# A written-out order of all engines replaced by another one (with its buffer, PSUM and engine tables) in a gated mix of two long convolutions

## The chip, the cores and the metric

The kernel runs on one core of one Trainium2 chip. A core has five engines that run at the same time, each through its own queue of instructions in a fixed order: TensorE (PE in the profile, its weight loads PEld) multiplies matrices into PSUM, VectorE (DVE) and ScalarE (ACT) work element by element on SBUF and PSUM, GpSimd (POOL) and SyncE (SP) here mostly issue DMAs. An instruction starts when it stands at the head of its engine's queue and the semaphores it waits for are set. The metric is the device time of one execution in microseconds (us), the median over several runs.

## What is computed

All arrays are bf16, the sequence has 2048 steps and there are 448 channels. The reference, cut to what matters:

```python
def _A_ref(u, A_re, A_im, B_re, B_im, C_re, C_im, log_dt, Dskip):
    dt = jnp.exp(log_dt)[:, None]
    logdA, dB = dt * (A_re + 1j * A_im), dt * (B_re + 1j * B_im)
    P = jnp.exp(logdA[:, :, None] * jnp.arange(L)[None, None, :])      # 448 x 256 modes x 2048
    K = jnp.einsum("dn,dnl,dn->dl", C_re + 1j * C_im, P, dB).real      # a filter of 2048 taps per channel
    return causal_convolution(u, K) + u * Dskip                        # by rfft, product, irfft of length 4096
def _B_ref(q, k, v, shift_k, ssm_k, ssm_D):
    kv = short_convolution_4_taps(k, shift_k) * v
    return q * (causal_convolution(kv, ssm_k) + kv * ssm_D)
x = A_u
g = sigmoid((x * gate_w).sum(-1, keepdims=True))
out = g * _A_ref(x, ...) + (1 - g) * _B_ref(x, k, v, ...)
```

## The kernel before, in words

**Tiling.** The 448 channels are four groups of 112. They lie on the partitions (32 per group) beside 32 residues of the sequence index, so that a sequence of 2048 is 32 x 64. The work on the filters goes through four channel quarters H = 0 to 3 of 28 columns x 4 groups (`NQG`, `NC`).

**Setup** builds constants with iotas on POOL and small DVE operations: tile `TP` serves as scratch, `G`, `s2_W` and `sa_R` (`s_W`, `sa_R` and `G` in the profile) are the transforms' matrices, `Wc` and `WcK` the masks. From dt, A, B and C it makes the modes' decay and phase (`hold`, q slots). Four of POOL's operations there fill 32x2048 elements each (method `turns`).

**The short convolution kv.** 448 matmuls in eight chunks of 56 multiply the transposed `k` (in tile `natu` and a slot) by a matrix `dg`, which is made on DVE in place in slot q1 from the `shift_k` load by two products (128x448 and 128x1344). Each chunk fills a PSUM room, and one DVE product `natv<-ps,natv` multiplies it by `v`. After the last chunk the four loads of `u` overwrite `natu`; the **gate** (112 matmuls `ps<-natu,q`, then tanh on ACT) reads `u`.

**A long convolution** of one quarter is a transform, a pointwise product and a transform back, all as matmuls: `spread` (`ps<-Wc,..`), `transform` (`ps<-q,s_W`), a swap of halves by eight SP DMAs (`q<-q`), two DVE products of 128x3584 (`q<-q,q`), `stage_a` (`ps<-sa_R,q`) and `stage_b` (`ps<-q,G`). After each PSUM room of results a copy (CAST or COPY `q<-ps`) brings it to a slot in bf16.

**A filter table T(H)** makes the filter K of one quarter: 16 exponentials on ACT (`q<-hold`), sines on ACT (`ET<-q`, with phases from DVE), a chain of DVE products and additions that builds the tables `TQ` and `TP` by doubling (`Part.tables`), with three accumulating POOL DMAs, then 448 small matmuls `ps<-TP,TQ` (`sums`), and a gather and spread on TensorE. Exponentials and sines use different function tables of ACT, and where the one follows the other the compiler puts an ACT_TABLE_LOAD between them.

**The plan** (`PLAN`) is T0 B0 B1 T1 B2 A0 T2 B3 A1 T3 A2, four mixes, A3 (A and B are the two convolutions of a quarter). T3 is made in two halves.

**What sets the order.** The Python code does not issue instructions: class `Order` records all 6479 calls in the order of the code, and `issue` (its line is L137, the one line that the trace has for all of them) then issues them as the string `ORDER` lists them (a number is a call, `a-b` a run of calls). Each engine's instructions are tied in that order, so no engine overtakes. Class `Places` hands out big buffers and PSUM rooms by two more strings: `SLOTS` gives for each request one of seven tiles q0 to q6 (128x3584 bf16), and `ROOMS` one of four PSUM tiles ps0 to ps3 (two banks each). A call that writes a slot or room waits until its earlier readers are done. Class `Sides` does the copies that DVE and ACT can both do: `SIDES` has one letter for each of 208 (V for DVE, S for ACT).

Calls by stage, for reading the diff: setup 0-226, kv 227-682 (its last product 682), loads of `u` 683-686, gate 687-804, T0 805-879, its sums 880-1327, gather and spread 1328-1448, B0 1449-1840, B1 1841-2237, T1 2238-2881 (sums 2313-2760), B2 2882-3278, A0 3279-3614, T2 3615-4259 (sums 3691-4138), B3 4260-4656, A1 4657-4992, T3 4993-5738, A2 5739-6074, mixes 6075-6078, A3 6079-6478.

Of the kernel before, what the change touches and what calls it, by code (L numbers as in the profile page):

```python
# [38 lines left out]
    "201031456232433120056615532041060303231061540604265013"  # L39
)  # L40
ROOMS = (
    "031230120122130132023010223312031201320001012121201100302332131110331210203301002313130323111031203103303210320132212000"
    "13111112310221033031032020012311212323010303033031323212102022201023121232131202010303130"
)
SIDES = (
    "SVSSSSSVSSSSSSSSSSSSSSSSSSSSSSSVSSSVSSVSSSSSSSSSSSSSSSSSSVVVVVSSSSSSSSSSSSSSSSSSSSSSSSSSSSSSSSSSSSSSSSSSSSSVVVVSSSSSSSSS"
    "SSSSSSSSSSSSSSSSSSSSSSVSSSSSSSSSSSSSSVSVVSVVSSSSSSVSSSSSSSSSSSVSSVVSSSSSSSSSVSVSVSSSVSSS"
)
ORDER = (
# [963 lines left out]
```

## Time and profile before

| what | value |
|---|---|
| median of 3 runs | 264.16 us (263.94 to 264.76) |
| profiled execution, first to last instruction | 257.9 us, so some 6.3 us of the measured time lie around it |
| DVE busy | 237.4 us in 378 instructions |
| TensorE busy | 208.9 us in 5631 matmuls |
| ACT busy | 199.5 us in 278 instructions |
| POOL busy | 30.5 us |
| DMA | 26.44 MB, mean 103 GB/s |
| first DVE operation, last DVE operation ends | 3.06 us, 247.6 us; what follows is the output's DMA |
| kv matmuls | 29.1 to 51.1 us |
| gate matmuls | 68.3 to 71.8 us |
| sums of T0, T1, T2 | 74.0 to 87.7, 121.5 to 132.5, 165.5 to 181.2 us |
| last matmul ends | 246.3 us |

All instructions have the line L137, so the profile is read by tiles: `q<-ps` is a copy out of PSUM, `TQ<-TQ,ET` a step of the filter's table chain, and so on. Buffer numbers are left out there (q stands for q0 to q6, ps for ps0 to ps3). Idle time of an engine stands with what ended it ("idle 11.67 <-PE ps": it waited for a matmul's room). Durations of DVE operations overlap by some hundredths of a microsecond, since the next one starts before the last one has written everything.

### The profile page before, as it was taken

How to read it: one execution, taken by the hardware profiler on the slowest of the kernel's cores; microseconds unless marked ns; L12 is line 12 of the kernel's file. 1: busy time of each engine (PE TensorE's matmuls, PEld its weight loads, DVE VectorE, ACT ScalarE, POOL GpSimd, SP SyncE). 2: the span in 40 equal slices, each digit the busy share in tenths (PEclk: the TensorE clock that was granted, in tenths of full speed). 3: DMA queues.
4: the chain of work that ended last, by engine and by line, in shares of the span. 5: the costliest groups of instructions: out<-in, count | busy, mean ns of one | idle time of the engine just before them, and what ended most of it. 6: DMA issues, size and time to landing. Idle time of an engine off the chain costs nothing.

```text
span 257.9 us, 12431 instructions
## 1 busy us (share of the span) xinstructions
PE 208.9 (81%) x5631; PEld 188.6 (73%) x5631; DVE 237.4 (92%) x378; ACT 199.5 (77%) x278; POOL 30.5 (12%) x81
## 2 busy tenths in 40 slices
PE   0634784988779999998889998989999998999820
PEld 0511484978669898997879887888899897998810
DVE  4999999999999999999999999988999999998830
ACT  2299993089979999999999999989999975653300
POOL 8970001200000002100000021000031120000000
PEclk9995596899979999999999999997999999999975
DMA  6999983499861347475043055600462375120088
GB/s 167 212 164 216 165 178 74 82 171 159 139 157 32 47 106 144 79 167 91 7 99 104 3 102 95 149 24 3 111 110 38 57 145 131 29 51 4 3 163 125
DMA packets 58917, 26.44 MB, mean 103 GB/s; under 512 B 49520, under 2 KB 57200, under 8 KB 58864
## 3 DMA queue, kind: packets, MB, share of 16 engines
q1 hardware_dynamic: 52192, 18.65, 39.5%
q0 software_dynamic: 2160, 5.51, 12.2%
q10 hardware_dynamic: 4512, 1.49, 3.0%
q8 instruction: 44, 0.72, 1.2%
q14 instruction: 9, 0.07, 0.1%
HBM read 8.17 MB, written 2.52 MB: 41 GB/s over the span
## 4 chain that ended last, share of the span: by engine, by line
DVE 61%; PE 17%; issue 6%; DMA 5%; ACT 5%; SPq 1%; POOL 1%; DVEq 0%; ACTq 0%; POOLq 0%
DVE TP L137 18%; PE ps L137 17%; DVE q L137 15%; DVE TQ L137 15%; DVE natv L137 5%; ACT q L137 3%; DMA TP<-TP 3%; DVE ET L137 3%; DVE G L137 2%; DVE RK L137 1%; SPq L137 1%; DMA q<-q 1%; ACT ET L137 1%; DMA sk<-in_B_ssm_k_dram 1%; DVE hold L137 1%
## 5 line engine op out<-in xcount | busy, mean ns | idle before, releaser
L137 ACT CAST q<-ps 128x1024 bf16<-128x1024 f32 (+4 forms) x151 | 126.6, 929 | 23.9 <-PE ps L137 23.1
L137 PEld LDWEIGHTS <-q 128*128 128x128 bf16 (+2 forms) x720 | 52.3, 147 | 13.5 <-DMA q<-in_A_A_re_dram 8.4
L137 DVE TENSOR_TENSOR TQ<-TQ,ET 128x896 bf16<-128x896 bf16 (+2 forms) x70 | 45.5, 687 | 0.1
L137 PEld LDWEIGHTS <-natu 128*32 128x32 bf16 (+1 forms) x560 | 30.6, 183 | 8.9 <-issue 7.2
L137 PE MATMUL ps<-TP,TQ 128*32 128x32 bf16 x1792 | 33.3, 240 | 4.1 <-DVE TQ L137 2.6
L137 PE MATMUL ps<-q,s_W 128*128 128x112 bf16 (+1 forms) x544 | 33.8, 214 | 3.5 <-ACT q L137 3.4
L137 PE MATMUL ps<-sa_R,q 128*128 128x128 bf16 x448 | 33.3, 229 | 2.4 <-DVE q L137 1.0
L137 PEld LDWEIGHTS <-TQ 128*32 128x32 bf16 x1792 | 30.1, 153 | 6.7 <-DVE TQ L137 3.1
L137 DVE TENSOR_TENSOR q<-q,q 128x3584 bf16<-128x3584 bf16 (+1 forms) x22 | 32.4, 1513 | 1.2 <-ACT q L137 1.2
L137 PEld LDWEIGHTS <-s_W 128*128 128x128 bf16 x544 | 28.2, 100 | 6.5 <-issue 4.5
L137 DVE TENSOR_TENSOR TP<-TP,ET 128x1792 bf16<-128x1792 bf16 (+3 forms) x25 | 31.4, 1275 | 0.1
L137 POOL DMA_DIRECT2D TP<-TP x15 | 13.1, 914 | 153.8 <-PE ps L137 89.6
L137 PEld LDWEIGHTS <-G 128*128 128x128 bf16 x1024 | 27.9, 96 | 4.3 <-issue 2.5
L137 PE MATMUL ps<-q,G 128*128 128x28 bf16 x1024 | 28.5, 175 | 1.4 <-ACT q L137 1.4
L137 ACT ACTIVATE q<-hold 128x224 bf16<-128x224 f32 x64 | 22.4, 414 | 5.0 <-DVE hold L137 5.0
L137 PE MATMUL ps<-q,natu 128*32 128x336 bf16 (+3 forms) x336 | 17.8, 334 | 5.7 <-DVE natv L137 4.2
L137 ACT ACTIVATE ET<-q 128x1344 bf16<-128x1344 int16 (+1 forms) x12 | 17.2, 1457 | 1.4 <-DVE q L137 1.3
L137 PE MATMUL ps<-q,q 128*32 128x336 bf16 (+3 forms) x112 | 17.8, 334 | 0.0
L137 PE MATMUL ps<-Wc,natu 128*64 128x128 bf16 x224 | 15.5, 285 | 0.6 <-DVE q L137 0.6
L137 ACT CAST RK<-ps 128x448 bf16<-128x448 f32 (+1 forms) x16 | 11.5, 742 | 5.4 <-PE ps L137 5.4
L137 DVE TENSOR_TENSOR TQ<-TQ 128x448 bf16<-128x448 bf16 (+2 forms) x35 | 15.3, 446 | 0.1
L137 DVE CAST q<-ps 128x1024 bf16<-128x1024 f32 (+3 forms) x13 | 12.6, 978 | 2.4 <-PE ps L137 1.4
(81 smaller groups left out, 276.6 us busy)
## 6 DMA issues: line engine op xcount, KB each, us to landing
q<-q SPq DMA_DIRECT2D x64, 112.0 KB, 3.1
TP<-TP POOLq DMA_DIRECT2D x9, 448.0 KB, 5.0
natv<-in_B_v_dram SPq DMA_DIRECT2D x4, 448.0 KB, 7.3
sk<-in_B_ssm_k_dram SPq DMA_DIRECT2D x16, 112.0 KB, 3.8
natu<-in_A_u_dram SPq DMA_DIRECT2D x4, 448.0 KB, 10.2
TP<-TP POOLq DMA_DIRECT2D x6, 224.0 KB, 3.8
out_dram<-natv SPq DMA_DIRECT2D x8, 112.0 KB, 4.6
out_dram<-natv ACTq DMA_DIRECT2D x8, 112.0 KB, 4.5
```

The lines of the kernel that those rows point to most:

```text
L137: ins = f(*args, **kw)
```

## The change

The calls are the same 6479, and so is all that they compute. The four strings are other ones: `SLOTS` and `ROOMS` place the buffers anew, `SIDES` has 22 letters V in place of 28, and `ORDER` issues the calls in another order on every engine. Some sums of a table (`1072-1135` before, `1072-1103` and `1104-1167` after, for instance) are cut at other places and stand among other groups of matmuls. The first lines are shown, and of `ORDER` those with the calls that the text speaks of:

```diff
@@ -36,71 +36,69 @@
 NSLOT = 7
 PLAN = (("T", 0), ("B", 0), ("B", 1), ("T", 1), ("B", 2), ("A", 0), ("T", 2), ("B", 3), ("A", 1), ("T", 3), ("A", 2), ("m", 0), ("m", 1), ("m", 2), ("m", 3), ("A", 3))
 SLOTS = (
-    "201031456232433120056615532041060303231061540604265013"
+    "011200652313211024454605234430165543031146525645042163"
 )
 ...
 SIDES = (
-    "SVSSSSSVSSSSSSSSSSSSSSSSSSSSSSSVSSSVSSVSSSSSSSSSSSSSSSSSSVVVVVSSSSSSSSSSSSSSSSSSSSSSSSSSSSSSSSSSSSSSSSSSSSSVVVVSSSSSSSSS"
-    "SSSSSSSSSSSSSSSSSSSSSSVSSSSSSSSSSSSSSVSVVSVVSSSSSSVSSSSSSSSSSSVSSVVSSSSSSSSSVSVSVSSSVSSS"
+    "SSSSSSSSSSSSSSSSSSSSSSSSSSSSVSSSSSSSSSSSSSSSSSSSSSSSSSSSSVVSVVSSSSSSSSSSSSSSSSSSSSSSSSSSSSSSSSSSSSSSSSSSSSVVVVSVSSSS"
+    "SSSSSSSSSSSSSSSSSSSSSSSSSSSVSVSSVSSSSSSSSSSVVVVVSSSSSSVSSSSSSSSSSSSSSSSSSSSSSSSSSSSSSSSSVVVS"
 )
 ...
 ORDER = (
-    "35 38 81 0 32-34 1 37 2 67-68 5 106 36 108 31 69 63 225 64 75 210 44 109 76 211 207 15 208 104 41 77 20 105 78 112 83 "
-    "107 74 6 71 202 70 66 212 72 209 73 221 214 50 82 30 65 111 219 110 79 17 140-155 215 84 216 116-117 203 222 91 204 "
 ...
-    "98-99 198 135 205 95-96 213 2257 206 125 200 101-102 136 826 47 92-93 126 838 128 97 138 218 114 341-396 843 835 139 "
 ...
-    "512-567 57 863 511 864 626-681 568 283 1466-1481 686 848 1449-1464 682 685 1483-1498 1465 684 850 1500-1507 1499 844 "
 ...
-    "1551 1535 868 2019-2026 1552 867 2246 1842 689-800 2027 1547 2018 1550 870 2239 1545 871 3615 872 879 1549 2259 877 "
-    "2037-2044 875 1621 2270 1136-1199 2269 2271 2260 2045 2264 1264-1327 2262 1845 2272 115 2263 2273 1640-1647 801 2265 "
-    "1008-1071 1648 2266 1880-1895 1897-1904 1896 880-943 1905 1649 1846-1861 802 1863-1878 2247 803 1072-1135 2243 2883 "
 ...
+    "2 15 71 1 19 67-69 75 77 116 70 104 72 109 207-208 105-106 108 111 209 112 225 76 33 214 63 28 212 60 210 107 110 "
 ...
+    "14 26 824 831-832 10 18 20 205 159 157 806 206 83 193-194 196 81-82 80 101-102 38 809 807 825-826 195 687 843 827 "
+    "198-199 89 130-135 137 136 98-99 74 833 45 139 123-124 120-122 125 39 95-96 200 2257 2238 50 129 812 46 839 814 127 "
+    "817 2240 128 819 828 197 834 92-93 138 73 47 49 846 126 808 848 835 847 850 94 849 852 840 103 841 512-567 48 97 "
 ...
+    "568 53 625 2253 55 54 398-510 341-396 855 52 682 201 57 2239 2244 2249 2258-2259 2243 41 511 227-283 683 685 "
 ...
+    "871 689-800 2037-2044 872 877 2241 1630 1648 867 2028-2035 801 2045 1844 864 869 1546 226 1631-1638 875 1613-1620 "
+    "1843 2036 802 876 1168-1231 1072-1103 1232-1295 2269-2270 2262 1639 944-1007 2271 2263-2266 2272-2273 2260 803 2251 "
+    "2267 1104-1167 1296-1327 3615 1329 3619-3620 1845 3626 880-943 1551 2274 1008-1071 3621 1552 3617 1880-1895 2261 "
 ...
```

What this does on the engines is shown at three places. In these lists q_77 to q_83 are the slots q0 to q6 and ps_84 to ps_87 the rooms ps0 to ps3; "x4" joins rows that read alike. The line is L135 after the change, as the strings are two lines shorter.

**DVE, the two products that make `dg`** (`q_78<-q_78,TP`, calls 74 and 73). Before they stand in the setup's first rows, among small constants:

```order
L137 TENSOR_SCALAR TP<-TP 128x32
L137 TENSOR_SCALAR TP<-TP 128x1
L137 TENSOR_SCALAR TP<-TP 128x64
L137 TENSOR_SCALAR TP<-TP 128x1
L137 TENSOR_TENSOR q_78<-q_78,TP 128x448
L137 TENSOR_SCALAR TP<-TP 128x1 x2
L137 TENSOR_SCALAR TP<-TP 128x4
L137 TENSOR_SCALAR TP<-TP 128x1
L137 TENSOR_TENSOR q_78<-q_78,TP 128x1344
L137 TENSOR_SCALAR minus<-TP 128x128
```

After, they stand behind the modes' products (`q_77<-TP`, `hold<-TP`) and among the products that make `G`:

```order
L135 TENSOR_TENSOR hold<-TP 128x8x2x28
L135 TENSOR_SCALAR G<-TQ,TP 128x64x32 x2
L135 TENSOR_TENSOR q_78<-q_78,TP 128x448
L135 TENSOR_SCALAR G<-TQ,TP 128x64x32
L135 TENSOR_TENSOR q_77<-TP 128x8x2x28
L135 TENSOR_SCALAR q_81<-hold 128x224
L135 TENSOR_SCALAR G<-TQ,TP 128x64x32 x3
L135 TENSOR_TENSOR hold<-TP 128x8x2x28
L135 TENSOR_TENSOR ET<-ET,q_83 128x3x448
L135 TENSOR_SCALAR G<-TQ,TP 128x64x32
L135 TENSOR_TENSOR q_78<-q_78,TP 128x1344
L135 TENSOR_TENSOR TQ<-hold,ET 128x896
```

So everything that DVE does in setup ahead of these rows now stands ahead of the matrix that the kv matmuls read.

**ACT, its first rows.** Before, the load of `shift_k` is ACT's first DMA, and two table loads stand ahead of the exponentials `q_81<-hold`:

```order
L137 DMA q_78<-in_B_shift_k_dram 128x1792
L137 DMA RK<-in_A_log_dt_dram 128x448
L137 ACT_TABLE_LOAD
L137 ACTIVATE TP<-TP 128x64
L137 ACT_TABLE_LOAD
L137 ACTIVATE TP<-RK 128x448
L137 ACTIVATE q_81<-hold 128x224 x2
L137 COPY RK<-ps_85 128x1792
L137 ACTIVATE q_81<-hold 128x224 x10
L137 ACTIVATE q_82<-q_82,quarter 128x4x224
L137 ACTIVATE q_83<-q_83,quarter 128x3x224
L137 ACT_TABLE_LOAD
```

After (from its sixth row on; two table loads stand ahead of these), there are table loads between the setup's sine for `sa_R` and the exponentials, and the load of `shift_k` has moved behind eight of ACT's operations on the exponentials and phases:

```order
L135 ACT_TABLE_LOAD
L135 ACTIVATE sa_R<-TP 128x256
L135 ACT_TABLE_LOAD
L135 ACTIVATE q_83<-hold 128x224 x4
L135 COPY RK<-ps_85 128x1792
L135 ACTIVATE q_83<-hold 128x224 x2
L135 ACTIVATE q_79<-q_79,quarter 128x3x224
L135 ACTIVATE q_83<-hold 128x224
L135 DMA q_78<-in_B_shift_k_dram 128x1792
L135 ACTIVATE q_83<-hold 128x224 x2
L135 ACTIVATE q_82<-q_82,quarter 128x4x224
L135 ACT_TABLE_LOAD
```

In all, ACT has 16 table loads after and 9 before. Ten of the 16 stand ahead of the first copy of B0's spreads; before, four of the nine do.

**ACT around T0's sums** (`RK<-ps` copies what they and no other matmuls leave, `gt` is the gate's tanh). Before, copies of B1's filter spreads (`q_78<-ps_84`, `q_78<-ps_85`) stand between the gate and the first copy of the sums:

```order
L137 ACT_TABLE_LOAD
L137 ACTIVATE q_82<-hold 128x224
L137 ACTIVATE gt<-ps_86 128x64
L137 ACTIVATE q_82<-hold 128x224
L137 ACTIVATE q_83<-hold 128x224
L137 COPY q_78<-ps_85 128x128x8
L137 ACTIVATE q_82<-hold 128x224
L137 ACTIVATE q_83<-hold 128x224
L137 ACTIVATE q_82<-hold 128x224
L137 COPY q_78<-ps_84 128x128x8
L137 ACTIVATE q_83<-hold 128x224 x2
L137 COPY RK<-ps_87 128x32x14
```

After, there are no copies of other matmuls between `gt` and the second copy of the sums, and those of B1's spreads come behind it:

```order
L135 ACT_TABLE_LOAD
L135 ACTIVATE ET<-q_83 128x3x448
L135 ACTIVATE ET<-q_77 128x3x448
L135 ACT_TABLE_LOAD
L135 ACTIVATE gt<-ps_86 128x64
L135 ACTIVATE q_82<-hold 128x224
L135 COPY RK<-ps_85 128x32x14
L135 ACTIVATE q_83<-hold 128x224 x6
L135 ACTIVATE ET<-ET 128x3x224
L135 ACTIVATE q_83<-hold 128x224 x3
L135 COPY RK<-ps_85 128x32x14
L135 COPY q_77<-ps_84 128x128x8
```

On TensorE the order has moved likewise: before, the sums of T0 stand in seven chunks of 64 with spreads, `transform` and `stage_a` groups between most of them; after, they stand in eight pieces of 64 or 32 with no other matmuls between.

More of the change, by code (lines that the diff above doesn't have):

```diff
@@ L38 @@
 SLOTS = (
-    "201031456232433120056615532041060303231061540604265013"
+    "011200652313211024454605234430165543031146525645042163"
 )
 ROOMS = (
-    "031230120122130132023010223312031201320001012121201100302332131110331210203301002313130323111031203103303210320132212000"
-    "13111112310221033031032020012311212323010303033031323212102022201023121232131202010303130"
+    "01231001012112100232101132130130121002331000202012103332132102313031210221220132300131001010302102012301102323203303"
+    "133000310220311032013302201202321002101113231232320031232013211122003013313201013310310202031"
 )
 SIDES = (
-    "SVSSSSSVSSSSSSSSSSSSSSSSSSSSSSSVSSSVSSVSSSSSSSSSSSSSSSSSSVVVVVSSSSSSSSSSSSSSSSSSSSSSSSSSSSSSSSSSSSSSSSSSSSSVVVVSSSSSSSSS"
-    "SSSSSSSSSSSSSSSSSSSSSSVSSSSSSSSSSSSSSVSVVSVVSSSSSSVSSSSSSSSSSSVSSVVSSSSSSSSSVSVSVSSSVSSS"
+    "SSSSSSSSSSSSSSSSSSSSSSSSSSSSVSSSSSSSSSSSSSSSSSSSSSSSSSSSSVVSVVSSSSSSSSSSSSSSSSSSSSSSSSSSSSSSSSSSSSSSSSSSSSVVVVSVSSSS"
+    "SSSSSSSSSSSSSSSSSSSSSSSSSSSVSVSSVSSSSSSSSSSVVVVVSSSSSSVSSSSSSSSSSSSSSSSSSSSSSSSSSSSSSSSSVVVS"
 )
 ORDER = (
[54 rows of a table removed]
[52 rows of a table added]
 )
```

91 rows, old and new, of the table ORDER are left out of this document.

## The prediction

> **What bounds the kernel now.** I read the page's head and chain first, then the busy time by stretches, then the waits, and last the timeline at the places that the change moves. From the page:
>
> ```profile
> span 257.9 us, 12431 instructions
> ...
> PE 208.9 (81%) x5631; PEld 188.6 (73%) x5631; DVE 237.4 (92%) x378; ACT 199.5 (77%) x278; POOL 30.5 (12%) x81
> ...
> DVE 61%; PE 17%; issue 6%; DMA 5%; ACT 5%; SPq 1%; POOL 1%; DVEq 0%; ACTq 0%; POOLq 0%
> ```
>
> DVE is busy for 92% of the span and is 61% of the chain that ended last. But the average hides that the limits differ by stage (columns: stretch, its length, then busy time of PE, weight loads, DVE, ACT and POOL):
>
> ```profile
> 40.00:60.00 20.00, 16.84 (x374) 15.51 (x375) 20.00 (x24) 8.24 (x13) 2.74 (x3) 0.83 0.77 120
> 80.00:200.00 120.00, 112.14 (x3125) 104.57 (x3122) 117.19 (x173) 116.41 (x164) 8.39 (x11) 0.99 0.40 81
> 100.00:180.00 80.00, 73.16 (x2124) 68.10 (x2122) 77.99 (x106) 77.57 (x106) 3.61 (x5) 0.98 0.39 82
> 200.00:246.00 46.00, 43.56 (x1349) 39.93 (x1348) 42.80 (x66) 26.48 (x35) 2.58 (x3) 1.00 0.29 61
> ```
>
> From 80 to 200 us DVE (117.2 of 120), ACT (116.4) and PE (112.1) are all close to full: ACT can make up at most 3.6 us there, and PE 6.8 between 100 and 180. From 40 to 60 and behind 200 ACT has room. Its largest idle time is one wait for kv:
>
> ```profile
> 52.48 3.99 ACT L137 CAST q<-ps 128x1024 bf16<-128x1024 f32 x4 [11.67 <-PE ps L137]
> ```
>
> So a delay of kv is one of the few things early on that ACT, and PE behind it, cannot hide: their work from there to 200 us is a row without gaps.
>
> **The change: kv starts later.** In the order before, `dg`'s two products are among DVE's first rows; in the new one the long one stands behind all products of the modes and seven of the eight `G` products. In the trace of before:
>
> ```profile
> 4.42 2.15 DVE L137 TENSOR_SCALAR TP<-TP 128x32 int32<-128x32 int32 x4
> 6.49 0.62 DVE L137 TENSOR_TENSOR q<-q,TP 128x448 bf16<-128x448 bf16 x1
> 7.02 1.56 DVE L137 TENSOR_SCALAR TP<-TP 128x1 int32<-128x1 f32 x3
> 7.54 1.55 DVE L137 TENSOR_TENSOR q<-q,TP 128x1344 bf16<-128x1344 bf16 x1
> 10.35 2.70 POOL L137 IOTA TP<- 32x2048 bf16 x3
> 10.50 1.87 DVE L137 TENSOR_SCALAR one<-TP 128x32 bf16<-128x32 int32 x1
> 15.56 2.90 ACT L137 ACTIVATE q<-hold 128x224 bf16<-128x224 f32 x10
> 31.59 2.08 DVE L137 TENSOR_SCALAR G<-TQ,TP 128x2048 bf16<-128x2048 bf16 x3
> 33.58 0.63 DVE L137 TENSOR_TENSOR TP<-TP,ET 128x896 bf16<-128x896 bf16 x1
> 34.11 0.86 DVE L137 TENSOR_TENSOR ET<-ET,q 128x1344 bf16<-128x1344 bf16 x1
> 37.32 0.63 DVE L137 TENSOR_TENSOR TP<-TP 128x896 bf16<-128x896 bf16 x1
> 40.89 1.09 DVE L137 TENSOR_TENSOR natv<-ps,natv 128x896 bf16<-128x896 f32 x1
> 42.89 0.63 DVE L137 TENSOR_TENSOR TQ<-hold,ET 128x896 bf16<-128x896 bf16 x1
> ...
> q<-in_B_shift_k_dram ACTq DMA_DIRECT2D x1, 448.0 KB, 5.4
> ```
>
> The seventh `G` product ends at 33.7 and the `ET` product, which is also ahead of `dg` now, at 35.0. Of what ran until then the 896 product (0.6) is not ahead; four small operations that ran later (0.2 to 0.3 each, together about 0.8) are. That is 35.2 us for the end of `dg`. The load of `shift_k`, now issued among ACT's first exponentials (they run until 18.5), lands 5.4 us later and is there by then. Unknown are POOL's big setup operations. While they run, small DVE operations last long: the one at 10.50 takes 1.87 us beside POOL's IOTA, and the groups at 4.42 and 7.02 show two more such stops. Before, the three cost DVE some 4.3 us together (2.15 + 1.56 + 1.87, less some 1.3 for seven or eight operations of 0.15 to 0.3); now the four POOL operations of about 1.9 us stand in one row at POOL's end, beside DVE's products of the modes. Bounds are no stop at all (4.3 us earlier) and all four in full (3.3 later). The operations are the same ones, so I take the cost near the old, 0.8 more for their standing in one row: kv starts at 36, where it started at 29.1.
>
> How long it then takes, by chunks of 56 matmuls (the last columns are the clock granted to PE, the DMA share and GB/s):
>
> ```profile
> 29.10:32.30 3.20, 3.18 (x60) 2.80 (x63) 3.20 (x8) 3.20 (x5) 0.00 (x0) 0.50 1.37 166
> 32.10:34.50 2.40, 2.40 (x71) 2.19 (x67) 2.40 (x5) 2.40 (x3) 0.00 (x0) 0.74 1.37 217
> 34.30:36.20 1.90, 1.90 (x75) 1.90 (x72) 1.90 (x4) 1.87 (x3) 0.00 (x0) 1.00 0.87 282
> ...
> 37.90:42.00 4.10, 0.00 (x0) 0.00 (x0) 4.07 (x6) 2.92 (x7) 1.01 (x1) 0.78 0.02 3
> 42.00:45.20 3.20, 3.17 (x60) 2.80 (x63) 3.20 (x3) 0.00 (x0) 0.00 (x0) 0.50 0.79 148
> 45.00:47.70 2.70, 2.70 (x71) 2.36 (x67) 2.70 (x5) 0.00 (x0) 0.87 (x1) 0.63 0.11 21
> 49.20:51.10 1.90, 1.90 (x72) 1.84 (x66) 1.90 (x3) 0.00 (x0) 0.86 (x1) 1.00 0.29 56
> ```
>
> Four chunks fill the rooms in 3.2 + 2.4 + 1.9 + 1.9 = 9.4 us (the first at a clock of 0.50, the fourth like the third). PE then waits 4.1 us for DVE's first `natv` product (40.89, ending 42.0) and starts again at 0.50. In the new order DVE has 17 products between `dg` and that one, table products but for one `G` (the first is the row at 42.89, the last but one that at 37.32, and each takes 0.38 to 1.10). That is 11.6 us of durations, or 10.6 from start to start as neighbours overlap by some 0.06: the first `natv` product ends at 47.7, and PE, done with four chunks at 45.4, waits 2.3. With the slow clock again after that wait, the other four take 3.2 + 2.7 + 1.9 + 1.9 = 9.7 and kv ends at 57.4 (51.1 before): 6.3 us late.
>
> The Trainium skill ("TensorE: Matmul & The Clock Gate", Part 1) says that the clock falls back to half only after an idle window of about 3.4 us. The 4.1 us wait agrees; a 2.3 us wait would keep the clock by it, and kv would end 2.1 us earlier than I say, for 267.4 in place of 269.5 at the end. No run so far shows a wait of that length.
>
> What follows kv:
>
> ```profile
> 51.12 10.31 SPq L137 DMA_DIRECT2D natu<-in_A_u_dram  x4
> 68.27 3.56 PE L137 MATMUL ps<-natu,q 128*32 128x64 bf16 x112 [0.26 <-ACT q L137]
> 73.98 2.19 PE L137 MATMUL ps<-TP,TQ 128*32 128x32 bf16 x128 [1.65 <-DVE TQ L137]
> ```
>
> The loads of `u` go into the tile that kv reads, so they move by 6.3, and so does the gate, 68.3 to 74.6. PE idled 1.65 us before T0's sums for DVE's table; that gap takes up some, so PE's work is **4.7 us** late from there. With the bounds (kv start 4.3 + 0.8 earlier to 2.5 later, clock 2.1) it is between 0 and 7. DVE itself is hardly late: its operations until the end of T0 are the same apart from waits for kv's last two chunks (1 to 4 us).
>
> **T0's sums in one row.** 448 matmuls with none between give ACT nothing to copy for 448 x 2.19 / 128 = 7.7 us (by the row at 73.98), and B1's spreads come after. ACT has exponentials of T1 and T2 for some of it. The cost is between 0 and 3 us, and I take **1.0**, since most of it is work that ACT must do at some time.
>
> **Copies and table loads.** From the groups, with shapes kept apart, and the timeline of ACT at the gate:
>
> ```profile
> L137 DVE CAST q<-ps 128x1024 bf16<-128x1024 f32 x6 | 7.3, 1222 | 2.1 <-PE ps L137 1.1 <-ACT ET L137 1.0
> ...
> L137 ACT CAST q<-ps 128x1024 bf16<-128x1024 f32 x64 | 64.0, 1044 | 16.6 <-PE ps L137 16.2 <-DVE TP L137 0.3
> ...
> L137 ACT ACT_TABLE_LOAD x9 | 11.5, 1283 | 3.3 <-PEq L997 1.7 <-DVE q L137 1.4
> ```
> ```profile
> 79.02 0.60 ACT L137 CAST q<-ps 128x512 bf16<-128x512 f32 x1
> 79.63 1.28 ACT L137 ACT_TABLE_LOAD   x1
> 80.93 0.39 ACT L137 ACTIVATE q<-hold 128x224 bf16<-128x224 f32 x1
> 81.22 0.20 ACT L137 ACTIVATE gt<-ps 128x64 f32<-128x64 f32 x1
> ```
>
> DVE gives up three copies of 1024 (3 x 1.22), two smaller ones (some 0.65 each, by ACT's 0.60 for 512) and a tiny one (0.2), and makes one phase copy 0.1 longer: 5.1 us, or 4.7 as its operations overlap. ACT gains 4.4 us for the same copies. Its table loads go from 9 to 16, 7 x 1.28 = 9.0 us, but ten of the 16 stand ahead of B0's first copy (four before), where ACT had 11.67 us of idle time: six cost nothing, and one, 1.3 us, falls into the full stretch. If kv came early, that cover would be gone and they would cost up to 7.7. So ACT has 4.4 + 1.3 = 5.7 more there, and 3.6 of idle time against it: **2.1**.
>
> **The rest of the order.** B2's transforms and products come later, T1's and T2's sums stand among other matmuls, slots and rooms are other ones. All of that leaves each engine's amount of work as it is and can only change who waits for whom. The nearest row is what PE waits for ACT in all:
>
> ```profile
> PE ps L137 <- ACT q L137: 5.5, 18, 0.8
> ```
>
> I take nothing, with 5.5 us either way as the bounds.
>
> **What can be made up.** PE has 6.8 us idle between 100 and 180. It can use them only where DVE and ACT are ahead of it; ACT is not, so I take a third, **-2.5** (between 0 and -6.8). DVE's own 4.7 us less I count at nothing: DVE then waits for PE and ACT, which are late next.
>
> Sum: 4.7 + 1.0 + 2.1 - 2.5 = 5.3. The profiled execution of before has 257.9 us and some 6.3 around it, which is the median of 264.16; so 263.2 of span and **269.5 us**. Behind the last matmul stands the output's DMA, whose issues are not moved.
>
> **Rivals.**
>
> *DVE alone decides.* It is the chain's 61%, and it has 4.7 us less. If kv's lag is swallowed (POOL's stops vanish, the clock stays, so that the gate ends before DVE's table does), DVE's time counts: 264.2 - 4.7 + 1 to 3 for the waits at kv's end = 260.5 to 262.5. It decides if PE's lag at T0's sums is below about 1.7 us, which the gap of 1.65 can hide. Against it stands the row of windows: ACT is as full as DVE, and it gets the work that DVE loses.
>
> *They cancel.* Lag and lighter DVE give the same time within 0.8 us: 263.4 to 265.
>
> *ACT becomes the bound.* The lag of 4.7, T0's sums at their upper bound of 3, and 5.7 of added work with nothing made up: 13.4, at the most 277.6; I take 273 to 278. It decides if ACT stays over 97% busy until 200 us and waits elsewhere no longer. Against it: behind 200 ACT has 19.5 us idle.
>
> *A table load costs more than its own time.* It would, if ACT had to run empty around it. The rows at the gate show 0.01 us ahead of the load and 0.02 behind, and the overlap of 0.1 us that neighbours have (80.93 + 0.39 against 81.22) is lost: 7 x 0.1 = 0.7 us, a time inside the forecast's range. The Trainium skill ("ScalarE: Activation LUTs", What ACT_TABLE_LOAD costs) gives 1283 ns, as here, and about 1380 ns of drain besides. By that rule the seven would cost 9.7 us more than I say, at the worst 279; the rows at the gate show no gap of that size.
>
> **How the numbers follow.** Differences under 0.3% (0.8 us) could not be told from no change. The forecast (265 to 273) gets 0.56, DVE alone 0.20, cancelling 0.06, ACT as the bound 0.16, the dearer load 0.02. Faster is 0.20, same 0.06, slower 0.74. The range that leaves out no more than 2 in 10 reaches from 261 into ACT's case, 276; the forecast's own is 265 to 273.
>
> **What would show it.** In the profile after: first kv matmul near 36, a wait on `natv` of 2 to 3 us in mid-kv, kv's end near 57, gate near 75, T0's sums behind it in one stretch of 8 to 9 us (7.7 and some waiting); 16 table loads on ACT; DVE busy near 232 with more idle time "<-ACT q" and "<-PE ps"; the span near 263. I am wrong if kv starts before 32, if the gate comes before DVE's last `TQ`, or if PE is fuller than before between 100 and 180.

## The result, and the profile after

| kernel | median of its runs | against the kernel before on the same chip |
|---|---|---|
| after the change | 272.75 us (272.25 to 273.86) | 1.037 (1.031 to 1.043) |
| after the change, on another chip | 272.83 us | 1.033 (1.026 to 1.040) |
| before, run again as the kernel under test | 262.79 us | 1.001 (0.997 to 1.005) |

The change makes the kernel slower by 3.3 to 3.7%, some 9 us. The kernel before has medians of 261.8 to 264.1 us on these chips. Some executions take over 1% longer than the others of their kernel; the medians here leave them out, and the traces of the first cut and of the relief in the tail are of such executions. In each execution of which a span is known, the time is the span and some 1.8 us (272.25 for a span of 270.5 after, 262.56 for 260.7 before). So the execution profiled for the prediction, with its span of 257.9, was a quick one of about 259.7 us, and the "6.3 us around it" of the two texts above are not there. Below, the profile of before taken again (span 260.7) is compared with that of after; the shown one would make the difference 3 us larger than it is.

The page after:

```profile
span 270.5 us, 12420 instructions
...
PE 208.2 (77%) x5631; PEld 188.2 (70%) x5631; DVE 237.8 (88%) x372; ACT 214.6 (79%) x291; POOL 31.1 (11%) x81
...
PE 39%; ACT 16%; DVE 15%; SPq 10%; DMA 8%; issue 7%; POOL 0%; ACTq 0%; DVEq 0%; POOLq 0%
...
L135 ACT ACT_TABLE_LOAD x16 | 20.5, 1283 | 1.5 <-PEq L995 1.2
L135 DVE TENSOR_SCALAR q<-hold 128x224 int32<-128x224 f32 x40 | 16.3, 455 | 1.0 <-PE ps L135 1.0
```

and of before, taken again:

```profile
PE 208.5 (80%) x5631; PEld 188.0 (72%) x5631; DVE 237.7 (91%) x378; ACT 199.7 (77%) x278; POOL 30.6 (12%) x81
...
L137 DVE TENSOR_SCALAR q<-hold 128x224 int32<-128x224 f32 x40 | 10.1, 299 | 0.2
```

DVE has lost six copies and is as busy as before (237.8 against 237.7): its 40 phase operations `q<-hold` alone have grown from 10.1 to 16.3 us. DVE's share of the chain has fallen to 15% (48% in before again), PE leads it, and no engine is full. So the time has gone into waiting and into operations that stand still. The next table counts it on DVE, from its rows: when each filter table's last DVE operation ends, and how long DVE idled since the mark ahead of it (us; T3b is the second half of T3).

| DVE's mark | before again: end, idle | after: end, idle | lag |
|---|---|---|---|
| end of T0's table | 73.9, 3.7 | 78.2, 3.8 | 4.3 |
| end of T1's table | 124.2, 3.3 | 129.2, 7.0 | 5.0 |
| end of T2's table | 168.6, 0.2 | 177.4, 1.8 | 8.8 |
| end of T3b's table | 220.9, 2.9 | 229.2, 1.6 | 8.3 |
| last DVE operation | 250.5, 2.7 | 261.4, 9.4 | 10.9 |

Three stretches make the lag: 4.3 us up to the end of T0's table, 4.5 between there and T2's, 2.6 behind T3b, with 0.5 gained between T2 and T3b. A mark also moves when other operations are put ahead of it: between T1's and T2's the lag grows by 3.8 us, the idle time by 1.6.

PE's amount of work is a second measure (columns as in the prediction's windows). Before again and after:

```profile
0.00:80.00 80.00, 52.02 (x1159) 43.15 (x1160) 76.11 (x139) 56.77 (x81) 19.54 (x67) 0.87 0.89 152
0.00:200.00 200.00, 162.15 (x4243) 145.46 (x4245) 190.57 (x305) 170.78 (x241) 27.98 (x78) 0.94 0.60 109
```
```profile
0.00:80.00 80.00, 42.91 (x828) 35.45 (x832) 75.22 (x128) 60.22 (x85) 20.22 (x67) 0.97 0.78 139
0.00:200.00 200.00, 152.86 (x4033) 137.40 (x4034) 186.59 (x290) 174.05 (x239) 27.34 (x76) 0.97 0.56 107
```

By 80 us PE has done 9.1 us less than before, by 200 us 9.3 less. On PE the whole difference is there ahead of T0's sums, and from then on it neither grows nor shrinks much.

**The start.** POOL's four big operations now stand in a row, and DVE's small ones stand still beside them. POOL and then DVE after:

```profile
9.09 1.82 POOL L135 MEMSET TP<- 32x2048 bf16 x1
10.97 1.99 POOL L135 IOTA TP<- 32x2048 bf16 x1
13.00 1.83 POOL L135 MEMSET TP<- 32x2048 bf16 x1
14.89 2.70 POOL L135 IOTA TP<- 32x2048 bf16 x2
```
```profile
8.52 6.45 DVE L135 TENSOR_SCALAR q<-hold 128x224 int32<-128x224 f32 x6
14.89 2.00 DVE L135 TENSOR_SCALAR TP<-TP 128x4 f32<-128x4 int32 x1
15.02 2.71 DVE L135 TENSOR_SCALAR q<-hold 128x224 int32<-128x224 f32 x2
17.65 0.60 DVE L135 TENSOR_TENSOR hold<-ps,TP 128x448 f32<-128x448 bf16 x1
...
30.74 0.61 DVE L135 TENSOR_TENSOR q<-q,TP 128x448 bf16<-128x448 bf16 x1
...
37.58 1.55 DVE L135 TENSOR_TENSOR q<-q,TP 128x1344 bf16<-128x1344 bf16 x1
```

Nine operations, by the before row worth 0.15 to 0.3 us each, take DVE from 8.5 to 17.7. ACT waits for `hold` until 18.29, where its exponentials started at 13.45 before. Before again, ACT from there to its first sine into `s_W`:

```profile
13.45 0.67 ACT L137 ACTIVATE q<-hold 128x224 bf16<-128x224 f32 x2 [5.13 <-DVE hold L137]
...
20.15 1.28 ACT L137 ACT_TABLE_LOAD   x1
21.45 1.32 ACT L137 ACTIVATE ET<-q 128x1344 bf16<-128x1344 int16 x1
...
28.03 1.04 ACT L137 ACTIVATE s_W<-ps 128x1024 bf16<-128x1024 int16 x1
```

and after:

```profile
18.29 1.23 ACT L135 ACTIVATE q<-hold 128x224 bf16<-128x224 f32 x4 [7.42 <-DVE hold L135]
...
24.15 1.28 ACT L135 ACT_TABLE_LOAD   x1
...
32.03 1.28 ACT L135 ACT_TABLE_LOAD   x1
33.32 0.67 ACT L135 ACTIVATE q<-hold 128x224 bf16<-128x224 f32 x2
...
37.88 1.28 ACT L135 ACT_TABLE_LOAD   x1
39.17 1.02 ACT L135 ACTIVATE s_W<-ps 128x1024 bf16<-128x1024 int16 x1
```

That sine empties the PSUM room into which kv's first chunk goes. PE's first kv matmul, before again and after:

```profile
29.12 0.60 PE L137 MATMUL ps<-q,natu 128*32 128x448 bf16 x3 [1.49 <-ACT s_W L137]
```
```profile
40.24 0.60 PE L135 MATMUL ps<-q,natu 128*32 128x448 bf16 x3 [7.17 <-DMA natv<-in_B_v_dram]
```

It starts 0.05 us after the sine's end in both (28.03 + 1.04, 39.17 + 1.02). The row after names a DMA, a load of `v`, which landed at 40.23 and which these matmuls don't read. The transposed `k`, which they do read, was late as well: its transfer stood in SP's queue until 30.21 (17.11 before), as the slot q2 that it fills was T0's until ACT had read the phases. The trace doesn't have its landing; the second and third experiment tell it from the sine. kv thus starts 11.1 us later, where 6.9 were predicted.

**kv itself** went faster than predicted. First chunk, fourth, the wait and the second half, after (columns as in the prediction's windows):

```profile
40.20:43.20 3.00, 2.96 (x57) 2.54 (x60) 2.97 (x8) 3.00 (x3) 0.00 (x0) 1.00 1.38 159
...
47.20:48.80 1.60, 1.50 (x55) 1.37 (x48) 1.50 (x4) 1.60 (x6) 0.00 (x0) 1.00 0.04 10
48.80:50.60 1.80, 0.00 (x0) 0.00 (x0) 1.80 (x4) 1.80 (x5) 0.00 (x0) 1.00 0.00 0
50.60:52.20 1.60, 1.52 (x49) 1.52 (x52) 1.60 (x3) 1.57 (x3) 0.00 (x0) 1.00 0.00 0
...
55.60:57.30 1.70, 1.70 (x68) 1.70 (x60) 1.70 (x4) 0.00 (x0) 1.01 (x1) 1.00 0.03 10
```
```profile
50.68 0.43 PE L135 MATMUL ps<-q,natu 128*32 128x448 bf16 x3 [1.98 <-DVE natv L135]
```

The four first chunks take 8.5 us, the wait 2.0, the four last 6.8: no slow clock behind the wait. kv ends at 57.5, 7.1 later than before again (50.4) and where the prediction had it, but by luck, as errors of opposite sign met. The clock in the first of these rows needs care: it reads 1.00, but 57 matmuls in 3.0 us are as slow as before's 60 in 3.2 at 0.50.

**From kv to T1.** `natu<-in_A_u` follows kv and takes longer to land (median 11.3 us, 9.7 in before again), so that the gate, at 77.5 (74.6 predicted), is 9.2 us late where kv's end is 7.1 late. T0's sums run from 83.5 to 93.6. ACT waits for the gate, and its sines for T1, queued behind, are late for DVE:

```profile
77.50 3.56 PE L135 MATMUL ps<-natu,q 128*32 128x64 bf16 x112 [5.33 <-DMA natu<-in_A_u_dram]
```
```profile
81.11 0.21 ACT L135 COPY gx<-ps 128x64 f32<-128x64 f32 x1 [6.16 <-PE ps L135]
...
84.33 1.28 ACT L135 ACT_TABLE_LOAD   x1
85.62 2.55 ACT L135 ACTIVATE ET<-q 128x1344 bf16<-128x1344 int16 x2
```
```profile
86.98 0.86 DVE L135 TENSOR_TENSOR ET<-ET,q 128x1344 bf16<-128x1344 bf16 x1 [4.51 <-ACT ET L135]
```

### The profile page after: what moved, and what is told of

The parts are those of the page before. It is cut to its first block, busy times and chain, and to the rows that moved or that the text cites. A ratio compares the mean times of both kernels' runs of the same rounds, so it can differ in the third digit from the quotient of the medians.

```text
span 270.5 us, 12420 instructions
## 1 busy us (share of the span) xinstructions
PE 208.2 (77%) x5631; PEld 188.2 (70%) x5631; DVE 237.8 (88%) x372; ACT 214.6 (79%) x291; POOL 31.1 (11%) x81
## 4 chain that ended last, share of the span: by engine, by line
PE 39%; ACT 16%; DVE 15%; SPq 10%; DMA 8%; issue 7%; POOL 0%; ACTq 0%; DVEq 0%; POOLq 0%
PE ps L135 39%; ACT q L135 11%; SPq L135 10%; DVE q L135 6%; DMA natu<-in_A_u_dram 5%; DVE TQ L135 3%; DVE TP L135 3%; ACT ET L135 2%; ACT L135 1%; DMA q<-q 1%; DMA sk<-in_B_ssm_k_dram 1%; DVE RK L135 1%; DMA xfd<-q 1%; DVE natv L135 1%; ACT TQ L135 1%
## 5 line engine op out<-in xcount | busy, mean ns | idle before, releaser
L135 ACT CAST q<-ps 128x1024 bf16<-128x1024 f32 (+4 forms) x156 | 130.3, 927 | 19.1 <-PE ps L135 17.8
L135 PEld LDWEIGHTS <-q 128*128 128x128 bf16 (+2 forms) x720 | 51.7, 148 | 16.9 <-DMA q<-in_A_A_im_dram 6.7
L135 DVE TENSOR_TENSOR TQ<-TQ,ET 128x896 bf16<-128x896 bf16 (+2 forms) x70 | 45.3, 684 | 0.3
L135 PE MATMUL ps<-TP,TQ 128*32 128x32 bf16 x1792 | 34.1, 241 | 4.7 <-issue 3.3
L135 PEld LDWEIGHTS <-natu 128*32 128x32 bf16 (+1 forms) x560 | 29.0, 180 | 11.6 <-issue 10.1
L135 DVE TENSOR_TENSOR q<-q,q 128x3584 bf16<-128x3584 bf16 (+1 forms) x22 | 32.4, 1511 | 5.3 <-DMA q<-q 4.0
L135 PEld LDWEIGHTS <-TQ 128*32 128x32 bf16 x1792 | 30.7, 154 | 7.2 <-issue 5.0
L135 PE MATMUL ps<-q,s_W 128*128 128x112 bf16 (+1 forms) x544 | 32.2, 210 | 4.3 <-ACT q L135 4.1
L135 PE MATMUL ps<-sa_R,q 128*128 128x128 bf16 x448 | 33.2, 232 | 2.1 <-DVE q L135 1.6
L135 PEld LDWEIGHTS <-s_W 128*128 128x128 bf16 x544 | 27.1, 98 | 6.9 <-issue 5.1
L135 DVE TENSOR_TENSOR TP<-TP,ET 128x1792 bf16<-128x1792 bf16 (+3 forms) x25 | 31.5, 1271 | 0.1
L135 PEld LDWEIGHTS <-G 128*128 128x128 bf16 x1024 | 28.1, 96 | 4.2 <-issue 1.5
L135 PE MATMUL ps<-q,G 128*128 128x28 bf16 x1024 | 28.9, 174 | 1.2 <-ACT q L135 1.1
L135 POOL DMA_DIRECT2D TP<-TP x15 | 13.0, 868 | 146.0 <-PE ps L135 71.9
L135 ACT ACTIVATE q<-hold 128x224 bf16<-128x224 f32 x64 | 21.9, 406 | 7.5 <-DVE hold L135 7.4
L135 PE MATMUL ps<-q,natu 128*32 128x336 bf16 (+3 forms) x336 | 15.3, 301 | 9.1 <-DMA natv<-in_B_v_dram 7.2
L135 PE MATMUL ps<-TP 128*128 128x512 bf16 x16 | 7.7, 611 | 12.9 <-POOL TP L135 4.5
L135 ACT ACTIVATE ET<-q 128x1344 bf16<-128x1344 int16 (+1 forms) x12 | 17.4, 1458 | 0.1
L135 DVE TENSOR_SCALAR q<-hold 128x224 int32<-128x224 f32 x40 | 16.3, 455 | 1.0 <-PE ps L135 1.0
L135 PE MATMUL ps<-Wc,natu 128*64 128x128 bf16 x224 | 16.3, 287 | 0.1
L135 DVE TENSOR_TENSOR TQ<-TQ 128x448 bf16<-128x448 bf16 (+2 forms) x35 | 15.2, 444 | 0.2
## 6 DMA issues: line engine op xcount, KB each, us to landing
natu<-in_A_u_dram SPq DMA_DIRECT2D x4, 448.0 KB, 11.3
```

The lines of the kernel that those rows point to most:

```text
L135: ins = f(*args, **kw)
```

## The experiments

The theory at the outset was the prediction's: a late kv, by POOL's row on DVE and by what stands ahead of `dg`, sets the time, and what comes behind T0's sums is neutral. Its rivals were that the order behind T0 costs as much, that the table loads do, or that the measured execution of before was an odd one. In the diffs below only the numbers that move are shown; all else in the strings is as it was.

**POOL's big operations apart again, as before** (81, 83, 82 and 80 are the four).

```diff
 ORDER = (
-    "2 15 71 1 19"
+    "81 2 15 71 1 19"
...
-    "107 110 223-224 221"
+    "107 110 223 83 224 221"
...
-    "815 811 9 160-175"
+    "815 811 9 82 160-175"
...
-    "84 86 85 3 8 62"
+    "84 86 85 3 80 8 62"
...
-    "806 206 83 193-194 196 81-82 80 101-102"
+    "806 206 193-194 196 101-102"
```

> The new order with one thing undone: POOL's four big setup operations (32x2048) stand again early and apart in POOL's queue, as before, and not in one row at its end. In the profile of the new order DVE's small operations on the phases stand still beside them from 8.5 to 17.7 us, and the exponentials on ACT start at 18.3 (13.45 before). Theory 'a late start' (POOL's row holds the exponentials, these hold the last transpose of k and dg, so kv, the gate and T0's sums are late, and the lag stays to the end): exponentials near 13.5, kv's first matmul near 36, 268 to 269.5 us (3 to 4.5 less than the new order's 272.75). Rival 'the later order' (the lag of the start is made up, and what costs is how the stages from T1 on are interleaved): kv is earlier, the time 271.5 to 273.

Measured 269.5 us (268.1 to 271.2), 1.030 (1.025 to 1.035). DVE's phase operations are back at their old time and T0's table ends at 76.3 in place of 78.2:

```profile
L135 DVE TENSOR_SCALAR q<-hold 128x224 int32<-128x224 f32 x40 | 9.3, 280 | 2.5 <-PE ps L135 1.4 <-ACT ET L135 1.1
```

The exponentials start at 16.49 and kv at 38.45, both 1.8 earlier; 13.5 and 36 were expected. So POOL's row holds 1.8 of the exponentials' 4.8 us, and the other 3.0 stay. Others of DVE's operations now stand still, as they did before the change, so that its busy time falls by 2.9 us in all (237.8 to 234.9). Some 1 to 2 us of that reach the end (1.037 and 1.033 against 1.030, with intervals that overlap, so that this is likely and not certain).

**`k`'s transpose and `dg` early.** The transpose gets slot q4 in place of q2, T1's first phases change to q2 and move behind T0's, and `dg`'s products (74, 73) stand ahead of 843, a copy for T0's table.

```diff
 SLOTS = (
-    "011200652313211024454605234430165543031146525645042163"
+    "011400652313211024452605234430165543031146525645042163"
...
 ORDER = (
-    "837 2256 822 2254 830"
+    "837 822 830"
...
-    "21 2255 176"
+    "21 176"
...
-    "195 687 843 827"
+    "195 687 74 73 843 827"
...
-    "98-99 74 833"
+    "98-99 833"
...
-    "95-96 200 2257 2238"
+    "95-96 200 2256 2254-2255 2257 2238"
...
-    "92-93 138 73 47"
+    "92-93 138 47"
```

> The new order with kv's inputs undone: the last transpose of k gets slot q4 and T1's first phases get q2 (their first three DVE operations move behind T0's), so the transpose no longer waits for T0's sine on ACT; and dg's two products stand ahead of T0's table products. POOL's row stays. 'A late start': kv's first matmul moves from 40.2 to 33 to 36, its end from 57.5 to 51 to 54, the gate by 4 to 6; DVE's table for T0 still ends near 78, so T0's sums start 3 to 4 earlier: 268.5 to 270.5 us. 'The later order': 271.5 to 273.

Measured 273.76 us, 1.046 (1.042 to 1.049). kv was to start at 33 to 36 and started later instead, so the run says nothing on an early kv, but it shows what kv waits for:

```profile
29.65 2.10 DVE L135 TENSOR_TENSOR q<-q,TP 128x448 bf16<-128x448 bf16 x2 [3.27 <-DMA q<-in_B_shift_k_dram]
```
```profile
43.57 0.60 PE L135 MATMUL ps<-q,natu 128*32 128x448 bf16 x3 [13.23 <-ACT s_W L135]
```

`dg` was there at 31.8 and the transpose issued at 16.4, and kv still waited until 43.6, for ACT's sine into `s_W`, which the 3.3 us that DVE stood for `shift_k` had put off. So neither `dg` nor `k` was what kv waited for last.

**Both edits together.**

> Both of these together. 'A late start': kv starts near 30 to 32, T0's sums near 75 to 77, and the time falls to 264.5 to 267 us. 'The later order': 270 to 272, little less than with one of them.

Measured 270.88 us, 1.038 (1.031 to 1.044). kv starts at 39.94, right behind the sine into `s_W` (38.86 and 1.02 long), with `dg` done 11.8 us before:

```profile
39.94 0.62 PE L135 MATMUL ps<-q,natu 128*32 128x448 bf16 x3 [9.16 <-ACT s_W L135]
```

As kv moved by only 0.3 us, this run tells nothing between the two theories. In all fourteen profiles, those of the runs below included, the first kv matmul starts 0.05 to 0.06 us behind the end of that sine.

**The start as before, cut at four places.** The first 1171, 1786, 3095 or 5445 calls of the new order are put in the order, the slots, the rooms and the sides that they have in the kernel before; the rest stays as after. Each begins so, and goes over to the new strings at its place:

```diff
 ORDER = (
-    "2 15 71 1 19 67-69 75 77 116 70 104 72 109 207-208 105-106 108 111 209 112 225 76 33 214 63 28 212 60 210 107 110 "
+    "35 38 81 0 32-34 1 37 2 67-68 5 106 36 108 31 69 63 225 64 75 210 44 109 76 211 207 15 208 104 41 77 20 105 78 112 83 "
...
```

> The first 1171 calls that the new order issues (setup, kv, gate, T0's table and the first spreads of B0 and B1) stand in the order, slots, rooms and engines that they had before the change; all behind them stands in the new order. 'A late start': 263 to 266.5 us, close to the kernel before. 'The later order': at or above 269, since T0's sums in one row, B1's late spreads and everything from T1 on are still the new order's.

> The first 1786 calls of the new order (setup through T0's sums, B1's filter spreads and the begin of T1's table) stand as before the change, what is behind them in the new order. With the first 1171 calls as before, the ratio was 1.019. Theory 'contiguous sums' (T0's sums in one row and B1's spreads behind them hold ACT and DVE up): 1.005 to 1.010. Rival 'T1 and later': 1.015 to 1.022, no gain against the earlier cut.

> The first 3095 calls as before (through T1's sums and the begin of B2), the rest in the new order. 'T1 and later', if it is the stretch of T1 where B2's transforms wait behind T1's sums: 1.000 to 1.007. If the cost is the last stretch (DVE's waits for A2's swaps and for A3's copies, 3.5 + 2.5 + 1.2 us idle in the new order): 1.010 or more.

> The first 5445 calls as before (through most of T3), only the tail in the new order. If the waits of the tail are its own: 1.008 to 1.015. If they only pass on a lag from earlier: 0.997 to 1.004.

| as before up to | median, us | ratio to before | T1's, T2's, T3b's table ends, last DVE operation |
|---|---|---|---|
| 1171 calls, ahead of T0's sums | 266.58 | 1.019 (1.013 to 1.025) | 124.7, 174.8, 226.5, 259.1 |
| 1786, through T0's sums | 266.32 | 1.013 (1.008 to 1.018) | 122.3, 171.4, 224.8, 257.6 |
| 3095, through T1's sums | 268.64 | 1.021 (1.018 to 1.025) | 124.8, 173.9, 226.9, 259.0 |
| 5445, through the sums of T3's first half | 266.35 | 1.012 (1.009 to 1.016) | 124.3, 168.7, 226.7, 255.4 |

Putting the start back takes 1.4 to 1.8 points of the 3.3 to 3.7 away, 3.7 to 4.7 us. With T0's sums it is 2.0 to 2.4 points, and DVE is then as busy from T0 to T1 as it was. Busy time from 78 to 129 us (columns as above) of before again, after, and the second of these:

```profile
78.00:129.00 51.00, 46.01 (x1316) 42.67 (x1311) 47.66 (x58) 47.98 (x70) 2.59 (x3) 1.00 0.43 85
```
```profile
78.00:129.00 51.00, 45.05 (x1339) 42.32 (x1327) 44.03 (x57) 45.35 (x67) 2.56 (x3) 0.93 0.50 102
```
```profile
78.00:129.00 51.00, 44.15 (x1255) 41.16 (x1252) 48.08 (x66) 45.99 (x68) 2.56 (x3) 0.96 0.46 91
```

DVE's 3.6 us less in this stretch (44.03 against 47.66) come back with the old start and sums. But 1.3 points, some 3.4 us, stay with everything through T0's sums put back. What repeats behind them is the stretch from T1's table to T2's: 44.4 us in before again and in the last cut, which has the old order there, and 48.2 after and 50.1, 49.1 and 49.1 in the other cuts; DVE's idle time in it is 0.2 in before again and the last cut, 1.8 after, and 2.7 to 4.0 in the others. By what was expected, the first two cuts came out between the theories, and the last two where waits of the tail's own would put them. The cuts don't price either, since each seam makes a wait of its own: in the last one T3b's table ends 19.8 us behind T3's first half, against 13.3 in both kernels. How the 3.4 us fall on that stretch and on the tail stays open.

**After, run again; before, run again.**

> The changed kernel itself, unedited, beside the runs that follow: the anchor on this chip. Both theories: 1.037 times the kernel before (between 1.031 and 1.043).

> The kernel before, unedited, profiled anew: the profile shown of it has a span of 257.9 us, but the timed executions of it have spans of 258.5 to 262.2, with some 1.75 us around each. Ratio 1.00. If its profile was an ordinary execution, the new one has the same span and waits. If it was a lucky one: 260 to 262 us, and the places where the additional 2 to 4 us lie show how far the table of stages overstates the changed kernel's lag.

272.83 us and 262.79 us (the table above): the result holds on other chips, and the profile of before taken again, 2.8 us longer in span than the shown one, is the one to compare with.

**DVE's relief in the tail alone, in the kernel before.** Six copies behind T3 go to ACT, as the change has them:

```diff
 SIDES = (
-    "SSSSSSSSSSSSSSSSSSSSSSVSSSSSSSSSSSSSSVSVVSVVSSSSSSVSSSSSSSSSSSVSSVVSSSSSSSSSVSVSVSSSVSSS"
+    "SSSSSSSSSSSSSSSSSSSSSSVSSSSSSSSSSSSSSVSVVSVVSSSSSSVSSSSSSSSSSSSSSSSSSSSSSSSSSSSSSSSSVSSS"
```

> The kernel before with one part of the change done alone: six of the copies that the change takes off DVE (three of 1024, one of 896, two of 448, together 6.0 us), those that lie behind T3's tables, go to ACT; order, slots and rooms stay. Theory 'relief where DVE waits' (DVE is idle there anyway, so a lighter DVE is worth nothing): 0.997 to 1.003. Rival 'DVE bounds': 0.977 to 0.990.

Measured 261.44 us, 1.000 (0.996 to 1.004). DVE's busy time falls from 237.7 to 232.5:

```profile
PE 209.7 (80%) x5631; PEld 189.3 (72%) x5631; DVE 232.5 (88%) x372; ACT 204.3 (78%) x284; POOL 30.6 (12%) x81
```

and its idle time behind T3b rises from 2.7 to 8.9 us. In the kernel before, five microseconds less on the fullest engine are worth nothing there, and the same work more on ACT costs nothing. So much of the 9.4 us that DVE idles at the end of the kernel after may be no loss either; no run has tried it there.

**The gate behind two `transform` groups**, directly ahead of T0's sums, so that PE works while `u` comes; its copy, matmuls and tanh (801 to 803) go behind T1's last sine.

```diff
 ORDER = (
-    "871 689-800 2037-2044"
+    "871 2037-2044"
...
-    "2028-2035 801 2045"
+    "2028-2035 2045"
...
-    "1843 2036 802 876 1168-1231"
+    "1843 2036 689-800 876 1168-1231"
...
-    "2272-2273 2260 803 2251"
+    "2272-2273 801-803 2260 2251"
```

> The new order with the gate's 112 matmuls moved behind the last transforms of B0 and B1 (directly ahead of T0's sums), and the copy of its result on ACT behind T1's two sines. In the new order's profile PE waits 5.3 us for u, ACT 6.2 us for the gate, and DVE 4.5 us for T1's sines. If these three are one chain that is paid at the end: 1.020 to 1.028. If the stretch behind it absorbs them: 1.031 to 1.037, as unedited (1.033 and 1.037).

Measured 271.79 us, 1.038 (1.031 to 1.044), no gain. PE waits 1.22 us for `u` in place of 5.33 and T0's sums begin 2.5 us earlier, at 81.0. They end at 93.8 all the same, and DVE's wait for the sine is gone and has come back as others:

```profile
88.69 3.96 DVE L135 TENSOR_TENSOR q<-q,q 128x3584 bf16<-128x3584 bf16 x2 [2.30 <-DMA q<-q]
93.79 0.28 DVE L135 COPY TP<-ET 128x448 bf16<-128x448 bf16 x1 [1.14 <-PE ps L135]
105.96 1.09 DVE L135 TENSOR_TENSOR natv<-ps,natu 128x896 bf16<-128x896 f32 x1 [0.90 <-PE ps L135]
113.42 1.09 DVE L135 TENSOR_TENSOR natv<-ps,natu 128x896 bf16<-128x896 f32 x1 [1.29 <-PE ps L135]
115.57 3.96 DVE L135 TENSOR_TENSOR q<-q,q 128x3584 bf16<-128x3584 bf16 x2 [1.06 <-DMA q<-q]
```

So the gate's place is not the cause by itself: the time that one wait gives back goes into others.

**Three table loads less.** An operation of the setup (66) goes ahead of another (217), and T1's first phase copy and sine (2258, 2259) go to where the sines into `s_W` are.

```diff
 ORDER = (
-    "211 65 216 34 217 78"
+    "211 65 216 34 66 217 78"
...
-    "113 79 66 213"
+    "113 79 213"
...
-    "874 100 42 2242"
+    "874 100 2258-2259 42 2242"
...
-    "2244 2249 2258-2259 2243"
+    "2244 2249 2243"
```

> The new order with ACT's table loads cut from 16 to 13: in setup the two sines stand beside each other, and T1's first sine stands beside s2_W's. All three lie ahead of B0's first copy. If they are covered there: 1.031 to 1.037, as unedited. If a load is paid in full, 3 x 1.28 = 3.8 us: 1.018 to 1.023; with a drain of 1.38 more each, 8.0 us: 1.003 to 1.008.

Measured 271.67 us (271.54 to 272.51), 1.038 (1.031 to 1.045), no gain:

```profile
L135 ACT ACT_TABLE_LOAD x13 | 16.7, 1283 | 1.4 <-PEq L995 1.2
```

The loads that went stood in ACT's waits for `hold` and for kv's copies. The two that stand in ACT's row ahead of the first sine into `s_W` (32.03 and 37.88 after) were not taken away, since that would move T0's exponentials too.

**kv's start across the versions.** The six kernels that keep the new order behind the start can be put in a row by the start of kv: 38.45 (1.030), 39.94 to 40.87 (four kernels, 1.033 to 1.038) and 43.57 (1.046). So 5.1 us of kv's start go with 1.6 points, some 4.2 us of the time. The first and the last of these edits also change how long DVE stands, so this is a pattern and no proof.

No version among these is faster than the kernel before.

## Why the prediction was right, and where its terms were wrong

- **The side and the size.** Slower, by 3.3 to 3.7% (8.7 to 9.7 us); the prediction had 2.0% (5.3 us), and the measured 272.75 lies just inside the upper end of the forecast's own 265 to 273. What was short is named below.
- **kv starts late, and this is the largest part: right, for a wrong reason.** The step "kv starts at 36", by the end of `dg`, failed. kv started at 40.24 and waited last for ACT's first sine into `s_W`. The row of before had said so (`<-ACT s_W`). ACT's exponentials start 4.8 us late, 1.8 of it by POOL's row, and ACT then has 20.9 us of work ahead of that sine in place of 14.6, two more table loads (2.6) among it: 4.8 + 6.3 = 11.1, the measured lag.
- **POOL's row at 0.8 us: too small.** The nine operations beside it took 9.2 us, some 2 of it their own work (six took 1.50 in the first experiment), so about 7 us were standing still, where the prediction counted 4.3 for before: 2.7 more, inside the bound of 3.3. Undoing the row takes 2.9 us off DVE's busy time and is likely worth 1 to 2 us at the end, since other operations then stand still.
- **The clock behind kv's wait.** "With the slow clock again after that wait" failed: 6.8 us for the last four chunks in place of 9.7. The Trainium skill ("TensorE: Matmul & The Clock Gate", Part 1) lets the clock fall only after about 3.4 us of idle time. Both cases here agree: after 2.0 us the matmuls of 448 columns take 0.38 to 0.43 us, and behind 4.5 us in before again they take 0.58 from 0.9 us on. The prediction had the rule as the other value and chose the row of the longer wait. Its sums of the chunks were also 0.6 us too long each, as its windows overlap: without that, the first four chunks of before take 8.7 us (29.12 to 37.86) and the last four 9.1 (42.03 to 51.08). All this hid the error of the start of 4: kv's end, 57.4 predicted, came at 57.5.
- **PE's work 4.7 us late: too small.** The gate came 9.2 us late and not 6.3, as the loads of `u` also took longer, and PE had done 9.1 us less work by 80 us. T0's sums then start 9.6 us later than in before again and end 5.4 later, with fewer other matmuls between them. The old start is worth 3.7 to 4.7 us at the end, so the late start does not pay in full.
- **T0's sums in one row, 1.0.** They ran in one stretch of 10.1 us where 8 to 9 were told; the cut behind them is worth 0.6 points, 1.6 us, more than the cut ahead of them, with intervals that overlap. Inside the bounds of 0 to 3.
- **Copies and table loads, 2.1.** Six copies moved to ACT in the tail of the kernel before cost nothing, and three loads less gain nothing, so nothing shows this term. The statement that six of the extra loads cost nothing does not fit two of them: by the trace they lie in ACT's row ahead of kv's start (2.6 of the 11.1 us), which no run has tried. The Trainium skill's drain of some 1380 ns besides each load ("ScalarE: Activation LUTs", What ACT_TABLE_LOAD costs) does not show: after, each load but the first starts 0.02 us behind the operation ahead of it, and an operation that waits for nothing else starts 0.01 to 0.03 us behind the load, as at 32.03 and 33.32.
- **The rest of the order at 0, and 2.5 made up.** The 2.5 failed: PE's work is 9.1 us behind at 80 us and 9.3 at 200, and PE was hardly busier between 100 and 180 (72.4 us, 71.7 in before again), so no reserve was drawn on. The 0 failed as well: 3.4 us remain with everything through T0's sums put back. By the cuts the sum is 3.7 to 4.7 for the start, 1.6 for the sums and 3.4 behind, 8.7 to 9.7; it comes out by construction, as these are differences between neighbouring cuts. The parts are not independent either, since in the kernel after the whole lag is on PE ahead of T0's sums. That the later order costs behind an early start and hides behind a late one would fit both readings, but no run shows it.
- **DVE's 4.7 us less, at nothing: right**, by the experiment in the tail. Its forecast in the profile, "DVE busy near 232", failed: POOL's row alone gave DVE back 2.9 us of what the copies had freed (237.8 against 234.9).
- **Rivals.** DVE alone did not decide: its table for T0 was done at 78.2, PE came to the sums at 83.5, and DVE's share of the chain fell to 15%. ACT did not become the bound: 113.8 us of 120 busy from 80 to 200, no more than before. One sign of being wrong came by its words: the gate, at 77.50, starts ahead of the end of DVE's last `TQ` for T0 (78.2). It says little, as it does so before too (68.3 and 73.9). PE was fuller between 100 and 180 than in before again by 0.7 us, and less full than in the trace of the prediction (73.16).

## What to carry to other kernels

What starts a stage is the last of several releases, and the row of the kernel before names it: compute the arrival of that one in the new order first, and then of the others (here a PSUM room that ACT had to empty, a slot that a DMA had to wait for, and the operand itself). Relief of the fullest engine counts only in stretches in which it does not wait, so ask where in time the saved operations lie. And a reordered list that looks neutral in amounts should not be costed at nothing with a bonus for what may be made up: between engines that are all over 90% busy, a lag of 9 us on PE was still there at the end.

## What was not expected of the hardware

- Small operations of DVE stand still while POOL fills 32x2048 elements by MEMSET or IOTA: six phase operations of 128x224 took 6.45 us beside three of them, and 1.50 us in the kernel that has POOL's operations elsewhere:

```profile
13.93 1.50 DVE L135 TENSOR_SCALAR q<-hold 128x224 int32<-128x224 f32 x6
```

- The granted clock of a window can be wrong by a missing record: at the same place and with nearly the same number of matmuls (57 and 56) the profile after, whose clock records begin only at 43.9 us, has 1.00 and that of the kernel with the late gate has 0.50:

```profile
40.20:43.20 3.00, 2.94 (x56) 2.51 (x59) 2.97 (x8) 3.00 (x4) 0.00 (x0) 0.50 1.39 161
```

  The time of equal matmuls is the safer reading.
- One execution of the same kernel had a span 2.8 us shorter than another (257.9 and 260.7), a third of what the change costs. A lag read from two traces needs a second trace of each.
